# A packed attention and two MoE layers on one core: the first batch's v in tiles of its own, and both copies of turned probabilities on ScalarE

## The chip, the core and the metric

The kernel runs on one core of a Trainium2 chip. Times are device microseconds (us) of one execution; the figure of a kernel is the median of its runs.

## What is computed

The whole is an attention through a few packed rows, then a MoE layer in which every expert works on every row with a weight, then a soft MoE. Shapes: q, k, v (4, 8, 576, 64), p (4, 8, 32, 64); 2304 rows of 512 after the attention; 4 experts with 1024 hidden units in the first layer, 8 experts of 4 slots with 1024 in the second; all float32.

```python
def sm_attn(qq, kk, vv):
    s = scale * np.matmul(qq, kk.transpose(0, 1, 3, 2))
    a = np.exp(s - np.max(s, axis=-1, keepdims=True))
    return np.matmul(a / (np.sum(a, axis=-1, keepdims=True) + 1e-09), vv)
p_packed = sm_attn(p, k, v)
x = sm_attn(q, p_packed, p_packed)        # then (B*S, H*D)
...
for e in range(4):                         # first MoE
    out += prob[:, e:e + 1] * (np.maximum(x @ w1[e], 0.0) @ w2[e])
...
d = softmax(logits, over rows); c = softmax(logits, over slots)   # second: logits = x @ phi
out = c @ experts(d.T @ x)
```

## The kernel before

The order of the instructions is fixed by the Python program: each engine runs its own in the order in which they were written, and the framework adds the waits between engines by what each instruction reads and writes.

**Prologue (up to about 40 us).** `place_ops` orders the steps of the first batch's attention (its two groups of four heads, `attention(0, g, ...)` with `loads`), of the first expert weights (`make_g(0)`) and of turning the first layer's w2 (`wphi_ops`: PE turns a piece, L288; ScalarE puts it back, L295; PE multiplies by phi, L303) by costs written into each step, and calls them in that order. Loads are steps of SP, in this order: w2_0 in two halves, k of both groups (four loads), w2_1, v of group 0 (two loads), q of group 0 (two), v of group 1, q of group 1, w2_2, the first w1, w2_3. From then on ScalarE issues the w1 loads (L195).

An attention group goes: DVE turns k (L377), PE makes scores (`sa`, L391), DVE takes the maximum (L415, L418), ScalarE the exponentials (`ex`, L432, after a memset by GpSimd, L429), DVE normalizes them (L445 to L448), PE turns them in five pieces into two PSUM banks (`turn`, L454), the copies `et0` (four pieces, L462) and `et1` (the fifth, L468) bring them to SBUF, DVE turns q (L377 again), PE multiplies with v (`pv`, L490), ScalarE packs the result (L504, L507), PE makes the second scores (`sb`, L391), and DVE and ScalarE form the second softmax (L536 to L578) that ends in the operands of the expert products.

In the first batch all these buffers are places in one tile, `hr` (five places of 4608 columns, `flat[0]` to `flat[4]`), which later holds the hidden rows: q and turned k in place 0, v and `et` in place 1, turned q and the exponentials in place 2, w2 in places 3 and 4. v's loads write every second partition, since two loads share a tile:

```python
        for u in range(2):
            n = 4 if u and end else 5
            at = v.offset + (b * H + 4 * g) * S * D + 5 * D * u
            sp.dma_start(
                dst[u::2, :, : n * D],
```

`norm_probs` (L214 to L217, DVE) normalizes the domain probabilities with a scratch in `work`, a tile of six pieces of 576 columns; `spread_p` (GpSimd L712, DVE L715) then writes pieces 3 to 5 of `work`.

**Loop over 128 slots (to about 395 us).** 32 slots to a batch. A slot has twelve products of g with the attention's result (`mm1`, L659) into two banks, Relu by ScalarE (L669), the weight by GpSimd (L670) or both by DVE (L664), and a turn of the slot before into `hr` (L680). Every fourth slot makes the next g (L621, then ScalarE L633 and DVE L635) and the logits (L692). The next batch's attention runs beside it, one stage to a slot: group 0 from slot 8, group 1 from slot 13 of a batch, so the stage of `turn`, `et0` and `et1` stands in slots 14 and 19. PSUM has six banks for all of this, and a bank is used again when its reader is done.

**The rest.** Pooling (L823), then the second layer's experts, whose weights arrive in a stream of loads.

Of the kernel before, what the change touches and what calls it, by code (L numbers as in the profile page):

```python
# [18 lines left out]
def tile_packed_attention_moe_softmoe(  # L19
# [19 lines left out]
    pe, act, dve, pool, sp = nc.tensor, nc.scalar, nc.vector, nc.gpsimd, nc.sync  # L39
# [55 lines left out]
    def let_go(tiles):  # L95
        for i in [i for i, t in kept.items() if any(t is u for u in tiles)]:
            del kept[i]
            clock[0] += 1
            idle_since[i] = clock[0]
# [9 lines left out]
    cts = const.tile([128, S], F32, name="cts")  # L109
# [3 lines left out]
    flat = [hr[:, i].rearrange("p a b -> p (a b)") for i in range(RING)]  # L113
    work = const.tile([128, 6, S], F32, name="work")
# [34 lines left out]
    def load_v(b, g, t=None):  # L149
        if t is None:  # L150
            t = att_pool.tile([128, 4 * 5 * D], F32, tag="v", name=f"v{b}{g}")


        dst = t.rearrange("p (h x) -> p h x", h=4)
        end = (b, g) == (NB - 1, 1)
        if end:
            pool.memset(dst[:, :, 4 * D :], 0.0)
# [5 lines that stand above are left out]
                bass.AP(v.tensor, at, [[XR * D, 64], [S * D, 4], [1, n * D]]),  # L163
            )
        raw["v", b, g] = t
# [43 lines left out]

    def norm_probs():  # L210
        n = NB * NBLK
        s = sw("t0")[:, :n]
        v2 = dpn.rearrange("p b x e -> p (b x) e")
        dve.tensor_reduce(out=s, in_=v2, axis=AX.X, op=ALU.add)  # L214
        dve.tensor_scalar_add(s, s, EPS)
        dve.reciprocal(s, s)
        dve.tensor_tensor(  # L217
            out=v2, in0=v2, in1=s.unsqueeze(2).to_broadcast([128, n, NE]), op=ALU.mult
        )
# [48 lines left out]
    def load_w2(n, t, xs=(0, 4)):  # L268
        e, hf = divmod(n, 2)
        xs = slice(*xs)  # L270
        sp.dma_start(
            t[:, xs],
            w2[e, FC * hf : FC * hf + FC, :].rearrange("(x p) d -> p x d", p=128)[:, xs],
        )
        w2_t[n] = t
# [83 lines left out]
    def attention(b, g, tmp, late, gp, loads=None):  # L359

        ops = []
        st = {}
# [3 lines left out]
        def op(stage, eng, cost, *deps, take=0, give=0):  # L366
            def add(fn):
                ops.append(Op(stage, eng, cost, fn, deps, take, give))
                return ops[-1]
            return add  # L370
# [91 lines left out]
            act.copy(st["et"][:, 0:512], st["pt"][0])  # L462
            let_go(st["pt"][:1])

        @op(6, "DVE", 0.25, turn, et0, give=1)
        def et1():
            copy = act.copy if loads else dve.tensor_copy
            copy(st["et"][:, 512:640], st["pt"][1][:, 0:128])  # L468
            let_go(st["pt"][1:])

        et1.deps.remove(et0)
        et1.deps.append(turn)
        if loads:
            et1.eng, et1.cost = "ACT", 0.25

        @op(7, "DVE", 1.5, *landed("q"))
        def qf():
# [4 lines left out]
        @op(8, "PE", 1.6, et0, et1, *landed("v"), take=1)  # L482
        def pv():
            vt = raw.pop(("v", b, g)).rearrange("p (h x d) -> p h x d", h=4, d=D)
            ps = st["pv"] = mm_ps(f"pv{bg}", keep=True)
            for i in range(5):
                for hp in range(2):
                    for a in range(2):
                        c = 128 * i + 32 * (2 * hp + (a ^ g))
                        pe.matmul(  # L490
                            ps[64 * a : 64 * a + 64, 32 * hp : 32 * hp + 32],
                            vt[:, 2 * hp + a, i, :],
                            st["et"][:, c : c + 32],
                            start=(i == 0 and hp == 0),
                            stop=(i == 4),
                            skip_group_check=True,
                            tile_position=(0, 64 * a),
                        )
            late("v")
# [88 lines left out]
    def start_attention(b, g):  # L588
        if g == 0:
            flip_p(b)  # L590

        def late(stage):
            if stage == "k":
                for hp in range(2):
                    load_qk(q, "q", b, g, hp)
            elif stage == "v":
                if g == 0:
                    load_v(b, 1)
                elif b + 1 < NB:
                    load_v(b + 1, 0)  # L600
            elif b + 1 < NB:
                if g == 0:
                    load_p(b + 1)
                for hp in range(2):
                    load_qk(k, "k", b + 1, g, hp)

        return by_stage(attention(b, g, att_tmp, late, pool))
# [97 lines left out]
    def sw(tag):  # L705
        return work[:, ("t1", "la", "t2", "t0").index(tag)]
# [245 lines left out]
    with tc.manual_schedule():  # L952
# [7 lines left out]
        loads = {}  # L960
        ops = []

        def load(key, mb, fn, rank=0, deps=()):
            o = Op(0, "SP", 2.5 * mb, fn, deps, rank=rank)
            ops.append(o)
            loads[key] = o
            return o

        def load_two(src, nm, b, g, at=None):
            for hp in range(2):  # L970
                i = 2 * g + hp
                load_qk(src, nm, b, g, hp, at and at[:, S * i : S * i + S])
# [5 lines left out]
        load(("k", 0), 0.6, lambda: load_two(k, "k", 0, 0))  # L978
        load(("k", 1), 0.6, lambda: load_two(k, "k", 0, 1))
        load("w2_1", 1.05, lambda: load_w2(1, w2s[1]))  # L980
        load(("v", 0), 1.2, lambda: load_v(0, 0, flat[1][:, :1280]))
        load(("q", 0), 0.6, lambda: load_two(q, "q", 0, 0, flat[0]))
        load(("v", 1), 1.2, lambda: load_v(0, 1, flat[1][:, 1536:2816]))
        load(("q", 1), 0.6, lambda: load_two(q, "q", 0, 1, flat[0]))
        load("w2_2", 1.05, lambda: load_w2(2, w2s[2]))
        load("w1", 1.05, load_w1)
# [17 lines left out]
        def head_tmp(tag, name):  # L1004
# [11 lines left out]
        ops.append(Op(0, "DVE", 0.45, lambda: flip_p(0), ops[-1:]))  # L1016
        att0 = [
            attention(0, g, head_tmp, lambda stage: None, (dve, dve)[g], loads) for g in range(2)
        ]
        for g in range(2):  # L1020
# [12 lines left out]
        spread = spread_p(0)  # L1033
        ops.append(Op(0, "POOL", 1.5, copy_probs, [loads["k", 1]], rank=1))
        ops.append(Op(0, "DVE", 1.7, norm_probs, ops[-1:], rank=1))
        ops.append(Op(0, "POOL", 0.7, lambda: next(spread), ops[-1:], rank=1))
        ops.append(Op(0, "DVE", 0.77, lambda: next(spread), ops[-1:], rank=1))
# [75 lines left out]
        for s in range(nslot):  # L1113
# [26 lines left out]
            elif last == 8:  # L1140
# [8 lines left out]
                    op=ALU.add,  # L1149
# [18 lines left out]
        b = NB - 1  # L1168
# [257 lines left out]
```

## Time and profile before

| | us |
|---|---|
| median of the runs (lowest to highest) | 491.55 (490.72 to 492.34) |
| the profiled execution | 492.25 |
| its span | 490.4 |
| PE busy (share of the span) | 465.1 (95%) |
| DVE busy | 293.0 (60%) |
| ScalarE busy | 189.0 (39%) |
| GpSimd busy | 195.6 (40%) |

A row of a timeline gives the start, the time from the first start to the last end, the engine (SPq and ACTq: the queue's own instructions, such as the issue of a DMA), the line, what is written and read, and in brackets the idle time of the engine before it and what ended that. PE's granted clock was full in the stretches shown.

### The profile page before, as it was taken

The page shows a single profiled execution, that of the slowest core. Times are in us where ns is not written, and L with a number is a line of the kernel's source. Part 1 is how long each engine was busy: PE and PEld are TensorE (multiplying, and loading weights), DVE is VectorE, ACT ScalarE, POOL GpSimd, SP SyncE. Part 2 cuts the span into 40 slices and gives each one's busy share as a digit, 9 for nine tenths or more (in the row PEclk, how much of TensorE's full clock was granted, in tenths as well). Part 3 has the DMA queues.
Part 4 walks back from the last instruction along what each step waited for, and adds up shares of the span by engine and source line. Part 5 has one row for each costly group of instructions (what it writes and reads, how often), then busy time and mean ns, then how long its engine had stood idle before and what let it go on. Part 6 is the DMA issues. An engine that isn't in the chain of part 4 may idle for free.

```text
span 490.4 us, 13243 instructions
## 1 busy us (share of the span) xinstructions
PE 465.1 (95%) x5561; PEld 333.3 (68%) x5561; DVE 293.0 (60%) x553; ACT 189.0 (39%) x499; POOL 195.6 (40%) x257
## 2 busy tenths in 40 slices
PE   8779999999999999999999999999999998899993
PEld 6558777777776777778677777677788874422352
DVE  3585445787982687797568787882667642120022
ACT  3657554444441355454224445441434320020032
POOL 3002334455841644775335367751648512010000
PEclk9999999999999999999999999999999999999997
DMA  8699523745232345543205522243698679999997
GB/s 304 232 399 369 204 82 105 233 143 185 87 98 78 136 145 190 190 140 118 89 27 197 180 90 88 87 143 119 243 343 317 237 278 417 412 404 412 392 382 245
DMA packets 54140, 104.65 MB, mean 213 GB/s; under 512 B 5040, under 2 KB 20016, under 8 KB 54080
## 3 DMA queue, kind: packets, MB, share of 16 engines
q1 hardware_dynamic: 40416, 77.41, 43.1%
q10 hardware_dynamic: 13632, 26.35, 15.9%
q8 instruction: 44, 0.72, 0.6%
q14 instruction: 16, 0.13, 0.1%
q0 software_dynamic: 32, 0.04, 0.0%
HBM read 99.06 MB, written 4.72 MB: 212 GB/s over the span
## 4 chain that ended last, share of the span: by engine, by line
PE 72%; DVE 11%; DMA 10%; ACT 2%; issue 1%; POOL 1%; SPq 0%; ACTq 0%; DVEq 0%
PE h L659 34%; PE pb L823 8%; PE g L621 6%; PE lg L692 6%; DMA hr<-in_moe_w_dram 3%; PE w2t L288 2%; DMA wphi<-in_moe_w_dram 2%; DMA work<-in_moe_w_dram 2%; PE o L1380 2%; PE hid L1285 2%; PE pv L490 2%; DVE hr L680 2%; DMA w<-in_moe_w_dram 2%; PE si L1235 2%; DVE g L635 2%; PE sb L391 1%
## 5 line engine op out<-in xcount | busy, mean ns | idle before, releaser
L670 POOL TENSOR_TENSOR ht<-ht,work 128x288 f32<-128x288 f32 x191 | 155.5, 823 | 181.4 <-ACT ht L669 181.3
L659 PE MATMUL h<-a,g 128*128 128x288 f32 x1536 | 222.8, 300 | 0.6 <-DVE a L578 0.6
L659 PEld LDWEIGHTS h<-a,g 128*128 128x128 f32 x1536 | 206.6, 188 | 22.9 <-ACT g L633 11.8
L669 ACT ACTIVATE ht<-h 128x288 f32<-128x288 f32 x191 | 78.1, 412 | 150.9 <-PE h L659 137.9
L680 DVE STREAM_TRANSPOSE hr<-ht 128x576 f32<-128x576 f32 x128 | 97.6, 763 | 26.8 <-POOL ht L670 24.6
L635 DVE TENSOR_TENSOR g<-g,g 128x512 fp32r<-128x512 f32 x64 | 41.2, 684 | 36.3 <-ACT g L633 36.3
L633 ACT CAST g<-g 128x512 fp32r<-128x512 f32 x64 | 34.5, 589 | 20.4 <-PE g L621 20.4
L823 PE MATMUL pb<-hr,work 32*32 32x512 f32 x1152 | 40.0, 597 | 1.4 <-issue 1.4
L692 PE MATMUL lg<-ht,wphi 128*32 128x288 f32 x512 | 38.7, 412 | 0.0
L621 PE MATMUL g<-w,pkn 64*32 64x512 f32 x512 | 36.1, 601 | 0.9 <-DVE bm L556 0.6
L692 PEld LDWEIGHTS lg<-ht,wphi 128*32 128x32 f32 x512 | 14.0, 109 | 33.1 <-POOL ht L670 18.3
L664 DVE SCALAR_TENSOR_TENSOR ht<-h,work 128x288 f32<-128x288 f32 x65 | 28.2, 433 | 12.6 <-PE h L659 12.5
L823 PEld LDWEIGHTS pb<-hr,work 32*32 32x32 f32 x1152 | 23.2, 103 | 15.3 <-issue 6.5
L1323 DVE COPY ob<-o 128x256 f32<-128x256 f32 x12 | 4.7, 422 | 33.3 <-PE o L1380 33.3
L837 DVE SCALAR_TENSOR_TENSOR tacc<-tacc,rsc,pb 128x512 f32<-128x512 f32 x12 | 8.2, 744 | 26.7 <-PE pb L823 26.7
L288 PE MATMUL w2t<-ident,hr 128*128 128x128 f32 x128 | 19.6, 296 | 4.6 <-DMA hr<-in_moe_w_dram 2.5
L288 PEld LDWEIGHTS w2t<-ident,hr 128*128 128x128 f32 x128 | 17.5, 209 | 7.6 <-ACT hr L295 3.0
L295 ACT COPY hr<-w2t 128x512 f32<-128x512 f32 x32 | 17.8, 599 | 9.5 <-PE w2t L288 6.7
L712 POOL COPY work<-dpn 128x576 f32<-128x576 f32 x16 | 10.7, 666 | 7.1 <-DVE dpn L217 7.1
L122 PE MATMUL busy<-ident 128*128 128x128 f32 x77 | 12.0, 305 | 1.4 <-POOL ident masks.py:199 1.4
L122 PEld LDWEIGHTS busy<-ident 128*128 128x128 f32 x77 | 9.7, 156 | 4.9 <-issue 3.3
L715 DVE STREAM_TRANSPOSE work<-work 128x576 f32<-128x576 f32 x16 | 12.2, 761 | 0.0
(175 smaller groups left out, 422.7 us busy)
## 6 DMA issues: line engine op xcount, KB each, us to landing
w<-in_moe_w_dram ACTq DMA_DIRECT2D x25, 1024.0 KB, 5.2
ck<-in_moe_w_dram SPq DMA_DIRECT2D x38, 512.0 KB, 8.3
hr<-in_moe_w_dram SPq DMA_DIRECT2D x34, 512.0 KB, 8.2
hr<-in_moe_w_dram SPq DMA_DIRECT2D x7, 1024.0 KB, 7.8
w<-in_moe_w_dram SPq DMA_DIRECT2D x7, 1024.0 KB, 6.0
k<-in_k_dram SPq DMA_DIRECT2D x16, 288.0 KB, 5.1
v<-in_v_dram SPq DMA_DIRECT2D x11, 320.0 KB, 5.4
q<-in_q_dram SPq DMA_DIRECT2D x12, 288.0 KB, 3.7
```

The costliest lines, as they stand in the source:

```text
L122: pe.transpose(wp[:, :128], ident, ident)
L288: pe.transpose(st[x][:, 128 * dc : 128 * dc + 128], t[:, x, dc::NDC], ident,)
L621: pe.matmul(ps[g][c : c + 32, :], pkn_t[b][o : o + 64, g, hp, 0, :], t[o : o + 64, 2 * g + hp, :], start=True, stop=True, tile_position=(o ...
L633: act.copy(gg[:, 0, g], ps[g])
L635: dve.tensor_tensor(out=gg[:, 1, g], in0=ps[g], in1=gg[:, 0, g].bitcast(F32), op=ALU.subtract)
L659: pe.matmul(ps[:, :HS], gg[:, l, g, fs], m[:, ts], start=(g == 0 and i == 0), stop=(g == 1 and i == 2),)
L664: dve.scalar_tensor_tensor(out=ht[:, ts], in0=ps[:, :HS], scalar=0.0, in1=pr[:, ts], op0=ALU.max, op1=ALU.mult,)
L669: act.activation(out=ht[:, ts], in_=ps[:, :HS], func=AF.Relu)
L670: pool.tensor_tensor(out=ht[:, ts], in0=ht[:, ts], in1=pr[:, ts], op=ALU.mult)
L680: dve.transpose(out=hr[:, place(b, i), :, f0 : f0 + 32], in_=ht_t[s].rearrange("p (x t) -> p x t", t=32),)
L692: pe.matmul(lg_t[b][r][32 * x : 32 * x + 32, :HS], wphi[:, NFT * e + 4 * hf + x, :], ht_t[4 * ci + x][:, HS * r : HS * r + HS], start=(ch ...
L823: pe.matmul(pb[c][m : m + 32, :], d[o, x + par, :], hr[o, lo : hi + 1 : hi - lo, x + par, :], start=(x == 0), stop=(x == NBLK - 2), tile_p ...
```

## The change

v of the first batch's group 0 goes to the tile that the later batches' v use (`att_pool`, one buffer), v of group 1 to the first 1280 columns of `work`. The scratch of `norm_probs` goes from `work` to `cts`. `et1` is ScalarE's in all batches, not in the first alone; its dependence is the one it had.

```diff
     def norm_probs():
         n = NB * NBLK
-        s = sw("t0")[:, :n]
+        s = cts[:, :n]
...
-        @op(6, "DVE", 0.25, turn, et0, give=1)
+        @op(6, "ACT", 0.25, turn, et0, give=1)
         def et1():
-            copy = act.copy if loads else dve.tensor_copy
-            copy(st["et"][:, 512:640], st["pt"][1][:, 0:128])
+            act.copy(st["et"][:, 512:640], st["pt"][1][:, 0:128])
             let_go(st["pt"][1:])
 
         et1.deps.remove(et0)
         et1.deps.append(turn)
-        if loads:
-            et1.eng, et1.cost = "ACT", 0.25
...
-        load(("v", 0), 1.2, lambda: load_v(0, 0, flat[1][:, :1280]))
+        load(("v", 0), 1.2, lambda: load_v(0, 0))
         load(("q", 0), 0.6, lambda: load_two(q, "q", 0, 0, flat[0]))
-        load(("v", 1), 1.2, lambda: load_v(0, 1, flat[1][:, 1536:2816]))
+        load(("v", 1), 1.2, lambda: load_v(0, 1, work.rearrange("p a b -> p (a b)")[:, :1280]))
```

## Rows read from the trace of the kernel before

**Rows 1.** Busy by stretch (PE PEld DVE ACT POOL), clock, DMA share, GB/s: the loop.

```profile
40.00:400.00 360.00, 357.61 (x4312) 275.32 (x4311) 249.98 (x451) 153.53 (x400) 185.30 (x232) 1.00 0.46 160
```

**Rows 2.** Chain of waits in the prologue: start, us, what.

```profile
8.28 5.50 DMA hr<-in_v_dram
...
18.28 4.92 DMA hr<-in_q_dram
```

**Rows 3.** Timeline around the first exponentials.

```profile
12.02 0.21 DVE L418 TENSOR_SCALAR mx<-mx 128x1 f32<-128x1 f32 x1
...
13.88 0.41 ACT L432 ACTIVATE hr<-sa,mx 128x160 f32<-128x160 f32 x1 [2.21 <-DMA hr<-in_v_dram]
13.91 2.33 PE L288 MATMUL w2t<-ident,hr 128*128 128x128 f32 x16 [1.41 <-DMA hr<-in_v_dram]
13.92 0.25 POOL L429 MEMSET hr<- 128x64 f32 x2 [5.05 <-DMA hr<-in_v_dram]
```

**Rows 4.** Timeline of SP's queue: issues of loads.

```profile
7.51 1.37 SPq L161 DMA_DIRECT2D hr<-in_v_dram  x2
8.93 1.07 SPq L144 DMA_DIRECT2D hr<-in_q_dram  x2
16.96 1.27 SPq L161 DMA_DIRECT2D hr<-in_v_dram  x2
...
19.88 0.51 SPq L195 DMA_DIRECT2D w<-in_moe_w_dram  x1
...
47.47 1.28 SPq L161 DMA_DIRECT2D v<-in_v_dram  x2
```

**Rows 5.** Busy by stretch: the prologue's transfers.

```profile
2.50:14.50 12.00, 10.28 (x128) 7.24 (x128) 5.75 (x13) 4.57 (x11) 2.68 (x10) 1.00 1.05 383
14.50:19.00 4.50, 3.21 (x26) 2.57 (x25) 2.92 (x10) 4.50 (x20) 0.00 (x0) 1.00 0.13 25
19.00:52.00 33.00, 28.11 (x443) 22.86 (x446) 22.20 (x39) 20.36 (x52) 6.06 (x8) 1.00 1.04 375
```

**Rows 6.** Timeline from pv to the first h; last, PE's busy time alone.

```profile
18.94 1.36 PE L490 MATMUL pv<-hr 128*64 128x32 f32 x40
...
20.71 0.46 DVE L217 TENSOR_TENSOR dpn<-dpn,work 128x288 f32<-128x288 f32 x1
...
21.23 1.36 PE L490 MATMUL pv<-hr 128*64 128x32 f32 x40 [0.92 <-DMA hr<-in_v_dram]
21.24 0.66 POOL L712 COPY work<-dpn 128x576 f32<-128x576 f32 x1 [7.07 <-DVE dpn L217]
...
23.22 1.54 DVE L377 STREAM_TRANSPOSE hr<-hr 128x576 f32<-128x576 f32 x2 [2.05 <-DMA hr<-in_q_dram]
...
30.09 1.09 PE L621 MATMUL g<-w,pkn 64*32 64x512 f32 x16 [0.57 <-DVE bm L556]
...
32.93 0.75 DVE L556 TENSOR_REDUCE bm<-hr 128x18 f32<-128x576 f32 x1 [1.56 <-ACT hr L552]
...
39.78 1.84 PE L659 MATMUL h<-a,g 128*128 128x288 f32 x12
...
21.20:30.05 8.85, 7.18 (x153) 1.00 1.01 366
```

**Rows 7.** DMA issues up to 60 us: KB each, median us to landing.

```profile
w<-in_moe_w_dram SPq DMA_DIRECT2D x1, 1024.0 KB, 10.1
```

**Rows 8.** Line 468, `et1`: ns min/median/max.

```profile
L468 DVE COPY et<-et x6: 253/268/282, 88.6 to 287.5; 128x128 f32<-128x128 f32 x6
L468 ACT COPY hr<-et x2: 271/308/344, 18.2 to 19.4; 128x128 f32<-128x128 f32 x2
```

**Rows 9.** Timeline of ScalarE: what stands behind `et0` in slots 14 and 19.

```profile
88.48 0.41 ACT L669 ACTIVATE ht<-h 128x288 f32<-128x288 f32 x1 [0.37 <-PE h L659]
...
103.26 0.41 ACT L669 ACTIVATE ht<-h 128x288 f32<-128x288 f32 x1 [0.32 <-PE h L659]
...
196.79 0.59 ACT L633 CAST g<-g 128x512 fp32r<-128x512 f32 x1 [0.29 <-PE g L621]
```

## The prediction

> **What bounds the kernel now.** I read the page first, where PE is by far the busiest engine, and then the busy time by stretches: from 40 to 400 us PE is busy for 357.61 of 360.00 us [rows 1], so the loop over slots has almost no gap to give back, and what ends before 40 us is worth its full length. (After 400 us the loads of the closing stages are issued as the loop lets go of their places, so they move with it.) The prologue is thus the part to read, and there the chain of waits is the next view [rows 2]. It is no chain of arithmetic: it goes from v's first load (5.50 us) to ScalarE's exponentials, from those to SP's issue of v's second load, on to a q load (4.92 us), DVE, PE's first g, and so to the first h at 39.78 [rows 6].
>
> The timeline shows why. VectorE has the first maximum ready at 12.02 + 0.21 = 12.23, but ScalarE's first exponential starts at 13.88, after 2.21 idle, and the row names the landing of v [rows 3]. The exponential neither reads v nor writes where v goes: it writes place 2 of hr, v lies in place 1. GpSimd's memset of the same buffer (13.92, after 5.05 idle) and PE's turn of w2 out of place 3 (13.91, after 1.41) name the same landing [rows 3]. A load of v writes every second partition; I infer that it is ordered against all of hr, earlier and later. The other direction is on SP: after q's first loads (8.93) the queue stands still until v's second pair goes out at 16.96 [rows 4]. In the chain that issue stands right behind ScalarE's exponentials, which again touch another place. Behind that pair stand q of the second group (18.28) and the first w1 (19.88) [rows 2, 4]. So the 16 DMA engines, at a share of 1.05 up to 14.5 us, are at 0.13 from 14.5 to 19.0, and then full (1.04) until 52 [rows 5].
>
> **The change part by part.** *v out of hr.* It removes these false waits and no instruction: the four loads of 320 KB stay, in their order on SP, to two other tiles. What it gives is bounded in two ways.
>
> By the transfers: from 19 to 52 us they run at their full share, so what the loads gain is the hole: 4.5 us x (1 - 0.13) = 3.9 us [rows 5]. SP has issued q's first pair by 10.0 and nothing on v's second pair waits for hr any more, so the queue is refilled before 14.5. All later landings then move by 3.9: v's second pair, which PE waited for until 21.23, to 17.3; q's, which VectorE waited for until 23.22, to 19.3; the first w1 (issued 19.88, 10.1 us to landing, so 30.0) to 26.1 [rows 4, 6, 7].
>
> By the engines: ScalarE's first exponential can start at about 12.3, 1.58 earlier. The first pv, at 18.94, stands at the end of that chain without a DMA wait, so it goes to 17.36; the second follows it on PE 1.3 later, at 18.65, instead of at 21.23, as its v is there at 17.3. From 21.20 to 30.05 PE has 7.18 us of work in 8.85 [rows 6]; with the gaps that were waits for q and w2 closed, PE comes to g at 18.65 + about 7.4 = 26.0. VectorE, which ends norm_probs at 20.71 + 0.46 = 21.17 and then waits 2.05 for q, ends it at 19.6 and goes on at once, q being there since 19.3: its run from 23.22 moves by 3.6. It would then be the later one by 0.3, but it has 1.56 of idle time ahead of 32.93, where it waits for ScalarE's second exponential of that stage; that one ScalarE's order puts behind the issue of the second w1, which waits for g (30.09) to have read the first [rows 6]. So g decides: PE can do it at 26.0, its w1 is there at 26.1, and it moves from 30.09 to about 26.2, by 3.9. From g to the first h the work and its order are the same: h goes from 39.78 to 35.9.
>
> Here a page speaks against a full gain. The trace has w1's first load at 10.1 us, while the w2 loads behind it were in flight [rows 7]. The Trainium skill, DMA: Bandwidth & Descriptors, section "Queues, rings and completion order", says that an engine takes turns between the queue rows at packet granularity and that a later descriptor may finish before an earlier one; what no run here has shown yet is how much an earlier start of more loads delays the one that is wanted first. By the row alone the sum stays 3.9. By that rule, with w1 as late as the w2 behind it, it is the second rival's, below.
>
> *v's new places.* The second piece lies in `work`, and if it is ordered against all of `work`, then GpSimd's spread of the probabilities (21.24, behind norm_probs) must wait for its landing at 17.3: covered by norm_probs (ending at 19.6), and if that cover were gone, the next to use it is the product of the first h at 40 us. norm_probs' scratch goes from `work` to cts: four instructions as before, no cost. The first piece lies in the tile that v of batch 1 takes next, so that load gets a new wait, for the first pv. SP issues it at 47.47, 27 us after that pv is over [rows 4, 6]; behind it on SP are loads of the next batch only. Nothing of before shows a transfer to these places in the prologue; nearest are v's loads into its own tile (47.47) and into hr. The bounds are from -0.5 us (v's first pair goes out up to a microsecond earlier than at 7.51) to +1.2 us (the SP time of a pair, 1.27, at a wrong moment [rows 4]). I take 0, as the DMA engines are full then.
>
> *The copy.* In the loop six copies of 128x128 go from VectorE (median 0.268 us) to ScalarE (0.308) [rows 8]; the prologue's two are on ScalarE already. Each stands behind the copy of the other piece, which waits for the same PE instructions, so no new wait arises; queued behind it is the next h's Relu, and PE waits for that Relu's bank. ScalarE is idle for 0.37 us ahead of that Relu at 88.48 and 0.32 at 103.26; in the second batch's later slot 0.29 is free ahead of the cast at 196.79 [rows 9], and the third batch repeats the second. So the copies are hidden, nearly to the last tenth: cost 0 to 6 x 0.03. On VectorE 6 x 0.268 = 1.6 us go, but PE idles for 2.4 us in all between 40 and 400 [rows 1], spread over many slots; if a tenth of that hung on these copies the gain would be 0.3, so 0 to 0.3. I take 0.
>
> **Sum.** 3.9 us (bounds 1.4 and 5.3) off the profiled 492.25 (span 490.4 and 1.85 around it) is 488.35. That execution lies 0.7 above the median of the runs, 491.55; the forecast is for the median: 491.55 - 3.9 = 487.65, rounded to **487.6**.
>
> **The rivals.**
> - *Forecast:* 3.4 to 4.3 us gone, 487.2 to 488.2. Chance 0.70.
> - *Transfers land out of turn:* g's w1 lands together with the w2 behind it, 1.05 MB or some 2.5 us later (1 MB at 375 GB/s gives 2.8 [rows 5]); the wait at g then takes the place of the one removed and the gain is 1.4 to 3.0 us: 488.5 to 490.1. For it: 10.1 us for one MB. Against: that long landing is already in the 30.0 that I moved. Chance 0.15.
> - *More than the hole:* the early start also takes slack from the first turns of w2, and h gains 4.4 to 5.3: 486.2 to 487.1. Against: the full DMA engines [rows 5]. Chance 0.07.
> - *It does not do what it says:* the ordering against hr comes from something else than v (the q loads into the same tile), and the waits only change their name: 491.5 give or take 0.7. For it: q follows v at once on SP, so the rows can't part them. Against: ScalarE's wait names v, and none of the three rows at 13.9 names q [rows 3]. Chance 0.05.
> - *Slower:* ScalarE's six copies come late to a Relu that PE needs. Place: slots 14 and 19 of the first three batches. The price is 0.31 each plus the bank's return, about 0.5, so 6 x 0.5 = 3.0, and it decides where it exceeds the 0.37 and 0.32 of idle time and the prologue gains under 1.5: 493.0 and more. Chance 0.03.
>
> **How the numbers follow.** The measurement of this kernel can tell about 0.3% (1.5 us) from no change. Faster by more than that: 0.70 + 0.07 + most of 0.15 = 0.91; within: 0.06; slower: 0.03. The range leaves out the last two cases and the ends of the others: 486.3 to 489.7.
>
> **What would show it.** Right: no wait for v at the exponentials, the memset or w2's turn; SP issuing v, q, w2 and w1 by some 16 us; no hole in the DMA share between 14.5 and 19; first h at 35.9 +- 0.5; from there each slot as far from the first h as before; the six copies on ScalarE, and the same 0.0 to 0.3 idle at the Relus. Wrong: g waiting for w1 beyond 27 (second rival), the exponentials still at 13.9 (fourth), or a Relu that ends later than before relative to its h, with PE's busy share in the loop below 99% (fifth).

## The result, and the profile after

The changed kernel takes 486.52 us (median; 485.67 to 489.39), the kernel before, run beside it, 491.50 (490.72 to 492.41): a ratio of 0.9902, 95% interval 0.9875 to 0.9929. 5.0 us are gone where 3.9 were forecast (487.6, range 486.3 to 489.7). Timed a second time its median was 486.49 and the ratio 0.9879 [0.9853, 0.9904].

| | before, us | after, us |
|---|---|---|
| median | 491.50 | 486.52 |
| profiled execution (span) | 492.25 (490.4) | 486.18 (484.4) |
| PE busy | 465.1 | 463.4 |
| first exponential | 13.88 | 12.35 |
| first g | 30.09 | 25.36 |
| first h | 39.78 | 35.06 |

In the code behind line 467 a line of after has a number smaller by three: pv is L487 (was L490), the first g L618 (L621), h L656 (L659). `et1` is L467 (L468).

First the timeline of after around the first exponentials, which answers to [rows 3]. Columns here and in all timelines: start, time from the first start to the last end, engine, line, what is written and read, and in brackets the idle time before it and what ended that.

```profile
8.54 0.25 POOL L429 MEMSET hr<- 128x64 f32 x2
...
12.10 0.21 DVE L418 TENSOR_SCALAR mx<-mx 128x1 f32<-128x1 f32 x1
12.35 0.41 ACT L432 ACTIVATE hr<-sa,mx 128x160 f32<-128x160 f32 x1 [0.59 <-DVE mx L418]
...
12.52 2.19 PE L288 MATMUL w2t<-ident,hr 128*128 128x128 f32 x16
```

No one waits for v any more: ScalarE starts as soon as VectorE's maximum is there, GpSimd's memset has moved up by 5.4 us, and PE's turn of w2 goes from 13.91 to 12.52. SP's queue of after, which answers to [rows 4]:

```profile
6.23 2.23 SPq L161 DMA_DIRECT2D v<-in_v_dram  x2
8.50 1.08 SPq L144 DMA_DIRECT2D hr<-in_q_dram  x2
9.63 1.27 SPq L161 DMA_DIRECT2D work<-in_v_dram  x2
10.95 1.76 SPq L144 DMA_DIRECT2D hr<-in_q_dram  x2
13.28 0.38 SPq L271 DMA_DIRECT2D hr<-in_moe_w_dram  x1
14.15 0.37 SPq L195 DMA_DIRECT2D w<-in_moe_w_dram  x1
```

v's second pair goes out at 9.63 instead of 16.96 and the first w1 at 14.15 instead of 19.88; the 7.0 us (10.00 to 16.96) in which SP stood still are gone. The busy time by stretch of after, which answers to [rows 5] (stretch, length, busy time of PE, PEld, DVE, ACT, POOL, granted clock, DMA share, GB/s), has no hole left, and the full stretch ends near 46 us instead of 52:

```profile
14.50:19.00 4.50, 3.17 (x66) 2.62 (x65) 3.88 (x10) 4.34 (x15) 0.00 (x0) 1.00 1.05 397
19.00:46.00 27.00, 25.03 (x374) 20.35 (x370) 19.42 (x34) 18.23 (x47) 5.81 (x8) 1.00 1.04 383
46.00:52.00 6.00, 5.67 (x80) 3.39 (x80) 2.15 (x4) 2.75 (x6) 1.84 (x3) 1.00 0.38 129
...
40.00:400.00 360.00, 357.83 (x4387) 274.65 (x4389) 247.90 (x444) 151.30 (x398) 183.38 (x230) 1.00 0.46 160
```

The timeline from pv to the first h, which answers to [rows 6]:

```profile
17.45 1.36 PE L487 MATMUL pv<-hr,v 128*64 128x32 f32 x40
...
18.64 1.34 PE L487 MATMUL pv<-hr,work 128*64 128x32 f32 x40
...
19.74 0.67 POOL L709 COPY work<-dpn 128x576 f32<-128x576 f32 x1 [10.95 <-DVE dpn L217]
...
25.36 1.09 PE L618 MATMUL g<-w,pkn 64*32 64x512 f32 x16
...
27.50 0.69 ACT L549 ACTIVATE hr<-hr 128x576 f32<-128x576 f32 x1
...
35.06 1.84 PE L656 MATMUL h<-a,g 128*128 128x288 f32 x12
```

The second pv follows the first at once, g waits for no load, and h stands 4.72 us earlier. The chain of waits of after (start, length, what) shows what is late now: up to the exponentials it is p's load and VectorE's turns, then ScalarE and PE, and no transfer of v or q is in it, unlike [rows 2]:

```profile
1.74 6.09 DMA p<-in_p_dram
...
12.35 1.45 ACT hr L432 x7
...
17.52 2.46 PE pv L487 x80
19.98 1.13 PE sb L391 x32
21.11 1.01 PE pw L303 x32
22.12 1.13 PE sb L391 x32
23.25 0.26 PE wp L319
23.50 1.93 PE w2t L288 x16
25.43 1.13 PE g L618 x16
```

After that the distance between the two traces hardly changes: 4.72 at the first h, 4.78 between 130 and 235 us, 4.80 at 320. Near 357 us it grows to 5.08, since a g of before waited for its weights there (0.21 us by its row at 362.48) and after's didn't (its row at 357.40). The rest of the profiled difference, up to 6.1 us, comes in the closing stages, which stand against their loads (DMA share 1.04 from 410 to 465 us in both); the medians differ by 5.0, so I don't count that rest as the change's.

### The profile page after: what moved, and what is told of

Same layout as the page of the kernel before. It is cut to its first block, busy times and chain, and to the rows that moved or that the text cites. A ratio compares the mean times of both kernels' runs of the same rounds, so it can differ in the third digit from the quotient of the medians.

```text
span 484.4 us, 13241 instructions
## 1 busy us (share of the span) xinstructions
PE 463.4 (96%) x5561; PEld 331.9 (69%) x5561; DVE 291.7 (60%) x547; ACT 189.6 (39%) x505; POOL 195.3 (40%) x257
## 3 DMA queue, kind: packets, MB, share of 16 engines
HBM read 99.06 MB, written 4.72 MB: 214 GB/s over the span
## 4 chain that ended last, share of the span: by engine, by line
PE 71%; DVE 11%; DMA 10%; ACT 3%; issue 1%; POOL 1%; SPq 1%; ACTq 0%; DVEq 0%
PE h L656 36%; PE pb L820 8%; PE g L618 6%; PE lg L689 6%; DMA hr<-in_moe_w_dram 4%; PE pv L487 2%; PE w2t L288 2%; PE sb L391 2%; DMA htck<-in_moe_w_dram 2%; PE o L1377 2%; DMA work<-in_moe_w_dram 2%; DVE hr L677 2%; DVE g L632 2%; DMA ck<-in_moe_w_dram 2%; PE sa L391 1%
## 5 line engine op out<-in xcount | busy, mean ns | idle before, releaser
L656 PE MATMUL h<-a,g 128*128 128x288 f32 x1536 | 222.7, 300 | 0.6 <-DVE a L575 0.6
L656 PEld LDWEIGHTS h<-a,g 128*128 128x128 f32 x1536 | 206.6, 188 | 22.8 <-ACT g L630 11.8
L618 PE MATMUL g<-w,pkn 64*32 64x512 f32 x512 | 36.1, 601 | 0.1
```

The lines of the kernel that those rows point to most:

```text
L618: pe.matmul(ps[g][c : c + 32, :], pkn_t[b][o : o + 64, g, hp, 0, :], t[o : o + 64, 2 * g + hp, :], start=True, stop=True, tile_position=(o ...
L656: pe.matmul(ps[:, :HS], gg[:, l, g, fs], m[:, ts], start=(g == 0 and i == 0), stop=(g == 1 and i == 2),)
```

## The experiments

Each is an edit of the kernel before or of the changed kernel, and each was timed beside the kernel before. Of the edits only the lines that matter are shown; `...` stands for lines left out. First h and first g are from its profile. The ratio is to the kernel before, with its 95% interval.

**Copy or v?** The kernel before with the copy alone moved:

```diff
-        @op(6, "DVE", 0.25, turn, et0, give=1)
+        @op(6, "ACT", 0.25, turn, et0, give=1)
         def et1():
-            copy = act.copy if loads else dve.tensor_copy
-            copy(st["et"][:, 512:640], st["pt"][1][:, 0:128])
+            act.copy(st["et"][:, 512:640], st["pt"][1][:, 0:128])
...
```

> The kernel before with only the copy moved: et1 is ScalarE's in all batches, v stays in hr. Theory (v's place is nearly all of the gain): first h at 39.8 as before, the loop 0 to 0.1 us shorter, median 491.4 within the measurement. Rival (the copies give a share, which would explain a gain of 5.0 where 3.9 was forecast): about 1 us faster, 490.4, spread over slots 14 and 19 of three batches.

Measured 492.12 us beside 492.03, ratio 0.9999 [0.9981, 1.0016]. The other half is the changed kernel with the copy back on VectorE in the loop (the same lines the other way round):

> The changed kernel with only v and the scratch moved; et1 is VectorE's in the loop as before. Theory: first h at 35.06 as in the changed kernel, median 486.5 to 486.7. Rival (the copies give 1 us): first h at 35.06, but each attention stage in the loop loses some tenths, median 487.5.

Measured 486.14 us, ratio 0.9870 [0.9847, 0.9894], first h at 35.22. So the new places of v are the whole gain, and the copy is neither gain nor loss. (The scratch of norm_probs moves along here; it also moves in the next run, which loses nearly all of the gain, so it isn't the cause.) The rows of one line (engine, count, ns least/median/most, first and last start) show why it costs nothing: on ScalarE the six copies of the loop take as long as they took on VectorE [rows 8]. This is `et1` in the changed kernel:

```profile
L467 ACT COPY et<-et x6: 268/270/274, 83.2 to 282.2; 128x128 f32<-128x128 f32 x6
```

The Relu behind them, at 88.48 with 0.37 us idle ahead of it before [rows 9], starts in after at 83.72 with 0.21 idle: 4.76 earlier, as far as everything else there.

**Which v?** Group 1's v back in hr, group 0's out of it:

```diff
-        load(("v", 1), 1.2, lambda: load_v(0, 1, work.rearrange("p a b -> p (a b)")[:, :1280]))
+        load(("v", 1), 1.2, lambda: load_v(0, 1, flat[1][:, 1536:2816]))
```

> The changed kernel, but v of group 1 is back in hr; v of group 0 has its own tile. Theory (a load of v is ordered against all of hr): the first exponentials start at 12.35 as in the changed kernel, but v's second pair again waits on SP for their end, at 15.4 instead of 16.96; the hole in the transfers stays, at 14.5 to 17.5; first h about 1.6 earlier than before, at 38.2; median 489.9. Rival (either pair alone ties everything): 491.5.

Measured 490.77 us, 0.9974 [0.9954, 0.9995]; exponentials at 12.24, first h at 39.26. The timeline shows SP's second v pair still held back, though by less:

```profile
15.36 1.27 SPq L161 DMA_DIRECT2D hr<-in_v_dram  x2
...
20.17 2.35 PE L487 MATMUL pv<-hr 128*64 128x32 f32 x40 [1.48 <-DMA hr<-in_v_dram]
```

And group 0's v back in hr, group 1's out:

```diff
-        load(("v", 0), 1.2, lambda: load_v(0, 0))
+        load(("v", 0), 1.2, lambda: load_v(0, 0, flat[1][:, :1280]))
```

> The changed kernel, but v of group 0 is back in hr; v of group 1 is in work. Theory: the exponentials wait for v again, to 13.9, so the engines' chain is 1.5 later than in the changed kernel, but SP does not stop before v's second pair and there is no hole from 14.5 to 19. If the engines decide the first g, it comes 1.5 later than in the changed kernel, at 26.9, first h at 36.6, median 488.1. If the transfers decide it, the first w1 lands at 25.2 as there, g and h move by less than 0.5: median 486.5 to 487.

Measured 487.90 us, 0.9908 [0.9881, 0.9936]; first g at 26.88 and first h at 36.58, as expected. The stretch from 14.5 to 19 has a DMA share of 1.05 and 398 GB/s, and yet h is 1.5 us later than in the changed kernel, because the exponentials are, by its timeline. Their row names VectorE's maximum, but that was ready at 12.38 (12.17 + 0.21); the row of PE's turn of w2, which starts with them, names v:

```profile
13.91 0.42 ACT L432 ACTIVATE hr<-sa,mx 128x160 f32<-128x160 f32 x1 [2.09 <-DVE mx L418]
13.94 2.33 PE L288 MATMUL w2t<-ident,hr 128*128 128x128 f32 x16 [1.29 <-DMA hr<-in_v_dram]
```

So the two waits are worth something each. The one on SP (group 1's v behind the exponentials) is the hole; with the hole closed, the one on ScalarE (exponentials behind group 0's v) still costs its 1.5 us in full. The run with group 1's v in hr lost more than its late load explains (h was expected at 38.2). Its first w1 had landed at 28.57 (issued 18.27, 10.3 us to landing), but PE came to g only at 29.56: the second pv took 2.35 us instead of 1.36, and from there to g PE was busy without a gap for 9.39 us, where the changed kernel needs 6.72. The last section comes back to that.

**Is it hr, or the shape of the load?** Here v stays in hr, both groups, but each load writes 64 adjoining partitions instead of every second one (the exponentials' order within a row is changed to match; copy and scratch as in the changed kernel):

```diff
-                dst[u::2, :, : n * D],
+                dst[64 * u : 64 * u + 64, :, : n * D],
...
-            ex = st["ex"].rearrange("p (i r t u) -> p i r t u", r=2, t=32, u=2)
+            ex = st["ex"].rearrange("p (i u r t) -> p i r t u", r=2, t=32, u=2)
...
```

> The changed kernel with both of v's groups back in hr, in the places of before, but each load of v writes 64 adjoining partitions (0 to 63, 64 to 127) instead of every second one; the columns of the exponentials are laid out to match, in all batches. Theory (the ordering against all of hr comes from the step over partitions): no wait for v at the exponentials, no stop on SP, first h at about 35.1, median 486.5. Rival (any load into hr beside other users ties them): as the kernel before, first h at 39.8, median 491.4.

Measured 491.49 us, 0.9984 [0.9966, 1.0001]; first h at 40.06. By its timeline the false waits are gone all the same:

```profile
9.71 1.26 SPq L161 DMA_DIRECT2D hr<-in_v_dram  x2
...
12.61 0.39 ACT L432 ACTIVATE hr<-sa,mx 128x160 f32<-128x160 f32 x1 [0.59 <-DVE mx L418]
...
21.12 2.35 PE L487 MATMUL pv<-hr 128*64 128x32 f32 x40 [2.05 <-DMA hr<-in_v_dram]
```

What it gained there it lost behind: first in the transfers, then on PE. By the busy time by stretch the transfers were never idle, but slow:

```profile
14.50:19.00 4.50, 3.16 (x54) 2.58 (x53) 3.82 (x12) 4.45 (x15) 0.00 (x0) 1.00 1.07 281
...
16.00:18.00 2.00, 1.25 (x18) 0.87 (x17) 1.86 (x5) 2.00 (x6) 0.00 (x0) 1.00 1.07 248
```

281 GB/s against the 397 of after in the same stretch at nearly the same share (1.05). The Trainium skill, SBUF — State Buffer, section "Door 1: The DMA port swizzle (why `[64,N]` ≈ `[32,N]`)", says that partitions 0 to 63 reach 8 of the 16 ports and 64 to 127 the other 8, so that a transfer over one of these halves gets about the rate of 32 partitions. The trace agrees in its direction (248 GB/s between 16 and 18 us while v flows), and the loads over every second partition, which by that section's table reach all ports, ran at 397. So the second pv starts 2.48 us later than in the changed kernel, and the first w1 lands at 28.27 (15.17 + 13.1). The other 2.52 of the 5.00 us by which h is later come on PE: from the second pv to g it is busy for 9.23 of 9.24 us, at a mean granted clock of 0.70, where the changed kernel takes 6.72 at 1.00. By its landing alone w1 would have let g start at 28.3 instead of 30.36; that is an estimate from this one trace. The three of the ten runs with the highest mean clock (0.991 to 0.993) still took 490.78 to 491.45 us, so how much of the median is the clock's stays open.

So this run parts the shape from the place as to the waits, not as to the time. The next load keeps both groups in hr and writes all 128 adjoining partitions, a head at a time, eight loads of 160 KB instead of four of 320 (from the changed kernel):

```diff
...
+            for hh in range(4):
+                sp.dma_start(
+                    dst[:, hh, :],
+                    bass.AP(
+                        v.tensor, at + hh * S * D,
+                        [[XR * D, 64], [5 * D, 2], [1, 5 * D]],
+                    ),
+                )
...
+        load(("v", 0), 1.2, lambda: load_v(0, 0, flat[1][:, :1280]))
...
+        load(("v", 1), 1.2, lambda: load_v(0, 1, flat[1][:, 1536:2816]))
```

> The changed kernel, but both groups' v stand in hr again (place 1, as before the change); each group is loaded head by head, four loads of 160 KB, each over all 128 adjoining partitions, so that no load steps over partitions. SP has eight v loads instead of four to issue; bytes and work of the engines are the same. If it is the step over partitions that orders a load against the whole of hr, and not hr as a place: first exponential at 12.3 to 12.7 without a wait for v, no hole in the DMA share between 14.5 and 19, a rate near 400 GB/s there (the halves on 64 adjoining partitions had 233 to 281), first h at 35 to 36.5, median 486.5 to 488. If any load of v into hr has to wait, whatever its shape: exponential at 13.9 or later, first h at 39 or later, 490.5 to 492.

Measured 487.22 us, 0.9897 [0.9865, 0.9929]. The exponentials stand at 12.16 and wait for the maximum alone, SP's second v goes out without a wait for them, as the timeline shows (its lines have numbers larger by 11 here):

```profile
10.69 3.26 SPq L169 DMA_DIRECT2D hr<-in_v_dram  x4
...
12.16 0.41 ACT L443 ACTIVATE hr<-sa,mx 128x160 f32<-128x160 f32 x1 [0.59 <-DVE mx L429]
```

With v in hr, and no new tile, the gain is the changed kernel's within the intervals. So it was the step over partitions, common to what both these runs undo, and not the place, that had the loads ordered against the whole tile; how the waits are worked out from the step is not in the record. Two of my numbers were missed: the rate from 14.5 to 19 was 304 GB/s, not 400, and first h 37.45, not 35 to 36.5, in a profiled execution that was itself the slowest of its runs (488.80, median 487.22). Why the rate fell (233 GB/s between 18 and 20 us at a share of 0.90) is open; four issues took SP 3.26 us where two took 1.27. The first w1 thus went out at 16.68 and landed at 26.48, and g came at 26.66, 1.30 later than in the changed kernel; the other 1.09 of h's 2.39 lie between g and h, behind a wait for w2 and at a lower clock (last section).

**Transfers or engines?** The changed kernel's first w1 in the list of DMA issues (KB each, median us to landing):

```profile
w<-in_moe_w_dram SPq DMA_DIRECT2D x1, 1024.0 KB, 11.0
```

So w1 has landed at 14.15 + 11.0 = 25.15 and PE comes to g at 25.36, and either could be the bound. The first w1 ahead of w2_2 on SP, the engines' order unchanged:

```diff
-        load("w2_2", 1.05, lambda: load_w2(2, w2s[2]))
-        load("w1", 1.05, load_w1)
+        load("w2_2", 1.05, load_w1)
+        load("w1", 1.05, lambda: load_w2(2, w2s[2]))
```

> The changed kernel; on SP the first w1 is loaded ahead of w2_2 instead of behind it, every engine's order the same. The first w1 lands at about 22.3 and w2_2 at about 25.2 instead of the other way round. If transfers are just in time (w2_2 is wanted at 23.3, w1 at 25.4), PE's turn of w2_2 now waits for its landing, about 1.9 us, g comes at 27.2, first h at 36.9, median 488.3. If the transfers have slack of 2 us or more and the engines alone decide, nothing moves: 486.5.

Measured 488.22 us, 0.9919 [0.9893, 0.9946]; g at 27.16, h at 36.87. In its timeline PE now waits for w2_2, which stands ahead of g in its order:

```profile
25.07 2.17 PE L288 MATMUL w2t<-ident,hr 128*128 128x128 f32 x16 [1.85 <-DMA hr<-in_moe_w_dram]
27.16 1.09 PE L618 MATMUL g<-w,pkn 64*32 64x512 f32 x16
```

The first w1 behind w2_3 instead:

```diff
-        load("w1", 1.05, load_w1)
-        load("w2_3", 1.05, lambda: load_w2(3, w2s[3]))
+        load("w1", 1.05, lambda: load_w2(3, w2s[3]))
+        load("w2_3", 1.05, load_w1)
```

> The changed kernel; on SP the first w1 is loaded behind w2_3 instead of ahead of it, every engine's order the same. The first w1 lands at 27.8 instead of 25.2. If g has no slack to its w1, as 25.2 against 25.4 says, g waits to 27.9 and first h comes 2.5 later, at 37.6, median 489.0. If landing order does not follow issue order (loads in flight share the engines), w1 lands less than 1 us later and the loss is under 1 us: below 487.5.

Measured 489.32 us, 0.9943 [0.9914, 0.9971]; h at 38.19, and g by the timeline:

```profile
27.63 1.96 PE L618 MATMUL g<-w,pkn 64*32 64x512 f32 x16 [2.33 <-DMA w<-in_moe_w_dram]
```

So a load that is one place later costs its transfer at once: there is no slack on that side. On the other side, p's loads ahead of phi's on ScalarE's queue give the engines an earlier start:

```diff
-        act.dma_start(phi_sb, phi.rearrange("(p c) s -> p c s", c=NDC))
         load_p(0, act, copies=1)
+        act.dma_start(phi_sb, phi.rearrange("(p c) s -> p c s", c=NDC))
```

> The changed kernel; ScalarE issues p's two loads ahead of phi's instead of behind it. In the changed kernel the chain of waits begins with p's second load, landing at 7.8, and VectorE's flips of k behind it. If that is the head of the chain and the engines decide, p lands up to 0.5 earlier and the first h moves by 0.3 to 0.5 at most as far as w1's landing at 25.2 lets it, so 0.2: median 486.3. If k's landing is as late as p's, nothing moves: 486.5.

Measured 486.55 us, 0.9882 [0.9856, 0.9908]. The exponentials came at 11.52, 0.83 earlier, but g at 25.12, only 0.24 earlier (no more than two profiles of the changed kernel differ by, with g at 25.36 and 25.59), as the second pv waited for its v, by the timeline:

```profile
18.38 1.36 PE L487 MATMUL pv<-hr,work 128*64 128x32 f32 x40 [0.44 <-DMA work<-in_v_dram]
```

Engines and transfers are thus level in the changed kernel: the exponentials made 1.56 later (group 0's v in hr) cost h 1.52, a load that PE wants made one transfer later costs g 1.8 or 2.3, and the engines made 0.83 earlier gain 0.24.

**Could h come earlier?** From the first g to the first h there are 9.69 us before, 9.70 in the changed kernel, and 9.70 or 9.71 in seven of the edits above (10.56 with w1 last and 10.79 with whole partitions, where the clock fell). p first (as in the edit just shown), w1 ahead of w2_2, and this time the order of the engines planned anew, so that g stands before w2_2's turn:

```diff
-        load("w2_2", 1.05, lambda: load_w2(2, w2s[2]))
         load("w1", 1.05, load_w1)
+        load("w2_2", 1.05, lambda: load_w2(2, w2s[2]))
```

> The changed kernel, with p's loads ahead of phi's on ScalarE, the first w1 loaded ahead of w2_2 on SP, and the order of the engines planned anew by that, so that PE makes the first g before it turns w2_2. Theory (the engines' work from the second pv to g decides, and 6.7 us stood there in the changed kernel): with the turn of w2_2 (2.3 us on PE) behind g, g comes 1 to 2 us earlier, at 23.4 to 24.4, if VectorE's and ScalarE's stages of group 1 allow it, and the first h at 33.3 to 34.5; median 485.0 to 486.0. Rival (the stages of the second softmax between g and h, and not g, set the first h, and the turn of w2_2 put between them delays them): first h at 35 to 36, median 486.5 to 487.5.

Measured 487.05 us, 0.9891 [0.9866, 0.9915]: the rival. g starts at 22.84, and h stands at 35.69. ScalarE's first exponential of the last stage (23.74 in after) now stands behind the issue of the second w1, which waits for g, and comes at 25.94; its second exponential is where it was (27.50 in after), since a cast of g and two copies now stand before it, as ScalarE's timeline shows:

```profile
25.42 0.39 ACTq L195 DMA_DIRECT2D w<-in_moe_w_dram  x1
25.94 0.68 ACT L549 ACTIVATE hr<-hr 128x576 f32<-128x576 f32 x1 [3.82 <-PE wp L319]
26.53 0.57 ACT L630 CAST g<-g 128x512 fp32r<-128x512 f32 x1
...
27.63 0.70 ACT L549 ACTIVATE hr<-hr 128x576 f32<-128x576 f32 x1
```

**The price of a stopped SP.** The second w1 issued by SP instead of ScalarE, so that ScalarE isn't held behind g (and p first):

```diff
-        (act if 0 < n < (NB - 1) * NCH + 2 else sp).dma_start(
+        (act if 1 < n < (NB - 1) * NCH + 2 else sp).dma_start(
```

> The changed kernel, with p's loads ahead of phi's on ScalarE and the second w1 issued by SP instead of ScalarE. In the changed kernel ScalarE's order puts its second exponential of the last stage behind that issue, which waits until the first g has read the first w1. Theory: that block costs the 0.3 to 0.5 us by which ScalarE starts late, so the first h comes at 34.3 to 34.6 and the median is 485.9 to 486.4. Rival (DVE and PE are as late by themselves): first h at 34.8 to 35.1, median 486.4 to 486.7.

Measured 492.32 us, 0.9995 [0.9974, 1.0015]: the whole gain is gone, and both my cases were wrong. I had freed ScalarE and not asked what stands behind the load on SP. It waits there until g has read the first w1, and the four w2 loads behind it wait with it, as the timeline shows:

```profile
16.08 0.59 SPq L271 DMA_DIRECT2D hr<-in_moe_w_dram  x1
...
26.48 0.37 SPq L195 DMA_DIRECT2D w<-in_moe_w_dram  x1
26.95 13.84 SPq L271 DMA_DIRECT2D hr<-in_moe_w_dram  x4
...
35.43 1.10 PE L288 MATMUL w2t<-ident,hr 128*128 128x128 f32 x4 [4.42 <-DMA hr<-in_moe_w_dram]
```

The busy time by stretch has the hole:

```profile
25.00:28.00 3.00, 1.73 (x22) 0.73 (x22) 2.86 (x7) 2.54 (x5) 0.00 (x0) 1.00 0.44 100
```

The DMA engines stand at 100 GB/s between 25 and 28 us, PE then waits 4.42 us for w2, and h comes at 40.75 (in a profiled execution of 494.9, 2.6 above that kernel's median). So this hole in the transfers, behind g instead of before it, is paid for as well. The changed kernel beside these three:

> The changed kernel itself once more, unchanged, to stand beside the last three on the same chip. Expected: first h at 35.1, median 486.5, ratio to the kernel before 0.988 to 0.992.

Measured 486.49 us, 0.9879 [0.9853, 0.9904], first h at 35.30. None of the edits is faster than it by more than the intervals.

## Why the prediction was right, and where its sum was off

**What it had right.** The bound (the prologue's waits, not the loop), the cause (v's loads with a step over partitions, ordered against all of hr in both directions), the place of the gain (the hole from 14.5 to 19 and the exponentials) and g as the point where transfers and engines meet are shown by the runs with half of v, with whole partitions, with w1's place changed and with the stopped SP. The engines' side of the first steps came out as worked out: exponential 12.35 (forecast 12.3), first pv 17.45 (17.36), second 18.64 (18.65), VectorE's turn of q at 19.59 without a wait for q (about 19.6).

**The two mis-sized terms.** I had g at 26.0 by the engines and at 26.1 by its load; it came at 25.36.

- *The hole.* I took 4.5 x (1 - 0.13) = 3.9 us from the DMA engines' busy share. In the hole of before that share moved 25 GB/s, while at a full share the engines move 375 in before [rows 5] and 397 in after. By bytes the hole is about (397 - 25) x 4.5 / 375 = 4.5 us, and the first w1 landed at 25.15 instead of 30.0, 4.85 earlier. Part of what is left lies right behind the hole: from 20 to 22 us the engines moved 292 GB/s in before and 410 in after. The share tells how long packets took and not what they moved: 0.13 at 25 GB/s, 1.05 at 397, and 1.07 at 281 with the halves over 64 partitions.
- *PE from the second pv to g.* I took 7.4 us, from a busy sum of 7.18 [rows 6] plus gaps. It took 25.36 - 18.64 = 6.72. There are no gaps in it (stretch of after, columns as above):

```profile
18.64:25.36 6.72, 6.72 (x159) 5.07 (x156) 6.38 (x12) 3.99 (x16) 0.67 (x1) 1.00 1.05 405
```

The busy sum of before was not all work that stays, either. The same groups of matmuls follow each other at once here, and each starts before the one ahead of it has ended: w2's turn took 2.16 us behind a wait in before, and here it adds 1.85 between the end of the product ahead of it (23.51) and g. The second sb took 1.20 instead of 1.33.

Both errors went the same way, by 0.95 and 0.7 us, so transfers and engines still met at g. That the two were alike is luck: 5.0 lies outside the 3.4 to 4.3 of the forecast's own case, and 486.52 is within the range because that reaches into the rival *More than the hole*. From g to h I forecast no change, 9.69 before and 9.70 after. The further 0.3 us or so of the loop (the wait for w1 at 362.48 that went) I had not seen.

**The unknown costs that I took as 0.** v's first pair went out 1.3 us earlier, and VectorE's maximum is ready at 12.31 instead of 12.23: 0.08 at most. The load of batch 1's v into the tile of the first piece goes out at 42.19, with its wait long past. GpSimd's spread of the probabilities starts at 19.74, right behind norm_probs and not held by v in `work`. The copies: 0.

**The rivals.**

- *Transfers land out of turn:* it needed g waiting for w1 at 27 or later. g's load did take longer (11.0 us against 10.1 [rows 7]) with the w2 loads behind it, but it was issued 5.73 earlier and landed before PE came. Not seen in the changed kernel; with w1 one place later the 2.33 us wait is there. The longer landing of w1, by 0.9 us, does not decide on the rule that spoke for this rival (the Trainium skill, DMA: Bandwidth & Descriptors, section "Queues, rings and completion order"): no run here shows two loads that changed places.
- *More than the hole:* its number is the one that came (486.2 to 487.1), yet its reason is not shown: the transfers gained 4.85 and the hole itself was larger than I reckoned, so h gained 4.72 with no slack in w2's first turns needed.
- *It does not do what it says:* refuted; q still goes to hr, and no wait for it is left at the exponentials.
- *Slower through the copies:* refuted by the copy alone.

## What to carry to other kernels

When waits name a load that touches other bytes, look at the shape of that load before its place: a step over partitions can have it ordered against the whole tile, in both directions, and here a whole-partition load of the same bytes freed it as well as a tile of its own (487.22 and 486.49 us, within the intervals). Size a hole in the transfers by bytes (GB/s in the hole against GB/s in a full stretch), not by busy share. Before a load is moved to another queue, ask what that queue still has behind it: a waiting load on SP brought back the whole 5 us.

## What the runs showed of the hardware that I had not expected

A wait of PE in the prologue can cost more than its length, as the granted clock falls to its lower level (0.50, 1.2 of 2.4 GHz). These are busy times by stretch of the run with v in halves, with the columns as above:

```profile
17.00:20.00 3.00, 2.02 (x45) 1.77 (x45) 2.84 (x6) 2.76 (x10) 0.00 (x0) 0.97 1.08 261
20.00:22.00 2.00, 0.88 (x17) 0.91 (x18) 0.53 (x1) 0.22 (x2) 0.66 (x1) 0.50 1.05 398
22.00:25.00 3.00, 3.00 (x60) 2.01 (x58) 0.95 (x2) 1.03 (x5) 0.00 (x0) 0.50 1.07 414
```

PE had been busy for 2.02 of 3 us, and at 0.50 then for 0.88 of 2; its second pv took 2.35 us where after has 1.34. The same pv took 2.35 with group 1's v in hr, the g behind the 2.33 us wait 1.96 instead of 1.09, with the second w1 on SP the clock was 0.50 from 35 to 40, after 4.42 us of waiting, and with whole-partition loads 0.51 from 29 to 32, after 1.39. The length of the wait does not tell which one does it: with w1 ahead of w2_2 PE waited 1.85 us and kept its clock at 1.00, and so did the kernel before behind its 0.92 [rows 6], in this stretch:

```profile
20.00:22.00 2.00, 1.08 (x39) 0.99 (x36) 1.10 (x3) 1.21 (x6) 0.66 (x1) 1.00 0.93 292
```

The price is more than the one slow instruction. In the two runs with the slow pv the clock was still 0.50 from 25 to 26 us, and PE took 2.52 and 2.67 us longer from that pv to g (9.24 and 9.39 against 6.72), without a gap; with w1 last, g took 0.87 longer and h stood 0.86 further behind it. The comparisons with these runs hold a part that is the clock's: the run with group 0's v alone out of hr came to 490.77 where 489.9 was expected, and its g started 1.0 us after its w1 had landed. That loads over 64 adjoining partitions ran at 248 to 281 GB/s, and over every second one at 397, was the other surprise; it would have hidden the cause, had the whole-partition load not been run.
